# A retention, mixing and gated-MLP kernel: four heads moved to the other half of the partitions, attention's state products in four quarters of the array, and no chunk turned by TensorE

## The chip, the cores and the metric

One core of one Trainium2 chip. The time is device microseconds for one execution of the whole program; lower is better. The kernel before takes 359.83 us (median of three runs, 358.95 to 359.85). The execution that was profiled took 360.07 us, of which 358.3 us lie between its first and its last instruction (the span); the other 1.8 us lie around them. Every time read from the trace counts from the start of the span.

## The reference

Three layers in a row, in float32, for 2 batches of 768 tokens; 8 heads of 64 make 512 features.

```python
def _attn_ref(q, k, v):                      # retention: linear attention with decay
    gamma = 1.0 - 2.0 ** (-5.0 - np.arange(H))
    for t in range(S):
        state = gamma * state + einsum('bhd,bhe->bhde', k[:, :, t], v[:, :, t])
        y[:, :, t] = scale * einsum('bhd,bhde->bhe', q[:, :, t], state)

def _moe_ref(x, w_theta, w_tok_r, w_tok_i, w_ch):
    theta = x @ w_theta
    zr, zi = x * cos(theta), x * sin(theta)
    y = einsum('ts,bsd->btd', w_tok_r, zr) + einsum('ts,bsd->btd', w_tok_i, zi)
    u = x + y
    return u + maximum(u @ w_ch, 0.0)

def _moe2_ref(x, ...):                       # 512 -> 1024, gelu, normed and gated over tokens, -> 512
```

## The kernel before, in words

**Stages.** Retention works on chunks of 128 tokens: 2 batches of 6 chunks, 12 in all. For a chunk, `scores` multiplies keys and queries of each head (contraction over 64 features, so one head uses 64 rows of TensorE's array), `mask` on VectorE copies them out of PSUM, `outer` makes this chunk's k-v product, `grow` (VectorE) and `shrink` (GpSimd) update the state, and `attend` adds up two products: queries with the state so far (only for chunks after the first of a batch: ten of twelve), and masked scores with values. `L682` (VectorE) multiplies the result with the decay `dq` and writes the features `x`. Then `theta` multiplies x with `w_theta`; sine and cosine come from ScalarE. They must be multiplied with x laid out by token, so x is turned: for chunks 0 and 1 (`TURNED`) TensorE transposes it (`turn`, L812); for the other ten, in pairs, VectorE transposes blocks of 32 (`by_token`, L715), one DMA writes them to DRAM (`scr`), and four DMAs bring them back. `mix_main` and `mix_rest` multiply with the token weights; two more stages of matrix products (channels, gated MLP) follow until the end.

**Precision.** The large products run as three fp32r products of high and low parts (`terms3`), so every x, z and weight is split by ScalarE (high part, L349) and VectorE (low part, L355). The small products of retention are plain fp32, and the trace records each of them as two passes: 8 matmuls appear as 16.

**Layout of the heads.** Eight heads are four pairs p; head h (0 or 1) of each pair has its 64 features in partitions 64h to 64h+63, for queries, keys and state alike.

**What sets the order.** `Plan` collects some 1,090 operations; `ORDER`, a list of their numbers, fixes the order in which each engine gets its own. Buffers come from fixed rooms (8 PSUM banks, 36 large SBUF buffers). Where the plan leaves TensorE idle early on, `keep_warm` fills the gap with products of `ident`. SP issues all loads in that order, and at most eight are under way.

Of the kernel before, what the change touches and what calls it, by code (L numbers as in the profile page):

```python
# [19 lines left out]
P = 128  # L20
NCH = S // P
NP = H // 2
# [19 lines left out]
TURNED = (0, 1)  # L42
# [26 lines left out]
class Plan:  # L69
# [171 lines left out]
def retention_spectral_gmlp(  # L241
# [286 lines left out]

    xhl, at = {}, {}
    zhl, z32 = {}, {}  # L530

    def retention(i):
# [12 lines left out]
        for pairs in steps:  # L545
            lo, hi = pairs[0] * P, (pairs[-1] + 1) * P

            def scores(pairs=pairs):
                for p in pairs:
                    for h in range(2):  # L550
                        rows = slice(h * D, (h + 1) * D)
                        cols = slice(p * P, (p + 1) * P)
                        q, k = part_of(qk, 0, p), part_of(qk, 1, p)
                        mm(ap(sc[h])[:, cols], k[rows], q[rows], True, True)
# [46 lines left out]
        if c < NCH - 1:  # L601
            kp = bank()

            def outer(pairs):
                for p in pairs:
                    for h in range(2):
                        rows, cols = slice(h * D, (h + 1) * D), slice(h * D, (h + 1) * D)
                        kk, vv = part_of(kv, 0, p), part_of(kv, 1, p)
                        mm(ap(kp)[rows, p * D : (p + 1) * D], kk[:, cols], vv[:, cols], True, True)
# [33 lines left out]
        xp = bank()  # L643

        def attend(pairs):
            a = ap(at[i])
            if c > 0:
                for p in pairs:
                    cols = slice(p * P, (p + 1) * P)
                    for h in range(2):  # L650
                        rows = slice(h * D, (h + 1) * D)
                        mm(
                            ap(xp)[rows, cols],
                            state[rows, p * D : (p + 1) * D],
                            part_of(qk, 0, p)[rows],
                            p == 0,
                            False,
                        )
# [911 lines left out]
```

## Time and profile before

| | |
|---|---|
| time, median of 3 | 359.83 us |
| the profiled execution | 360.07 us |
| its span | 358.3 us |
| TensorE busy | 353.4 us (99%) |
| VectorE busy | 286.0 us (80%) |
| ScalarE busy | 222.3 us (62%) |
| granted TensorE clock, mean | 1.000 (the 2.4 GHz level) |

Busy time is the union of an engine's instructions; those of TensorE are pipelined, so a pass lasts longer than the distance to the next. For prices the distance from the start of one run of equal passes to the start of the next is used below.

### The profile page before, as it was taken

What the parts mean: (1) busy time and instruction counts of PE and PEld (TensorE: products, weight loads), DVE (VectorE), ACT (ScalarE), POOL (GpSimd) and SP (SyncE); (2) the same over time, 40 slices, a digit from 0 to 9 for tenths busy, and PEclk for the clock granted to TensorE, in tenths of its full rate; (3) what the DMA queues carried; (4) which work ended last, traced back from release to release, by engine and by line L of the source; (5) the groups of instructions that cost most, each with busy time, mean ns of one, the idle gap of its engine ahead of it and who ended that gap; (6) DMA issues with size and microseconds to landing.
All of it is one profiled execution on the core that took longest, in us unless ns stands there. A gap on an engine that the chain in (4) does not pass through costs nothing.

```text
span 358.3 us, 5888 instructions
## 1 busy us (share of the span) xinstructions
PE 353.4 (99%) x2294; PEld 303.0 (85%) x2294; DVE 286.0 (80%) x468; ACT 222.3 (62%) x368; POOL 35.8 (10%) x47
## 2 busy tenths in 40 slices
PE   8999999999999999999999999999999999999996
PEld 8887887778899888889989888888888888999885
DVE  2799997989674786619799986989899794997993
ACT  2768976658561787484768679675698549236300
POOL 1111020000300030013021301000000003100000
PEclk9999999999999999999999999999999999999999
DMA  7999999149609056907559802911000015600344
GB/s 302 411 416 408 368 281 301 20 169 361 218 10 330 16 127 139 292 5 126 107 109 292 143 15 45 307 31 31 0 0 2 1 29 91 105 12 8 80 151 172
DMA packets 18123, 54.04 MB, mean 151 GB/s; under 512 B 2224, under 2 KB 5808, under 8 KB 15664
## 3 DMA queue, kind: packets, MB, share of 16 engines
q1 hardware_dynamic: 13776, 43.92, 34.3%
q0 software_dynamic: 4176, 9.70, 15.4%
q8 instruction: 18, 0.29, 0.3%
q14 instruction: 9, 0.07, 0.1%
q10 hardware_dynamic: 144, 0.05, 0.1%
HBM read 38.19 MB, written 5.77 MB: 123 GB/s over the span
## 4 chain that ended last, share of the span: by engine, by line
PE 89%; DMA 4%; DVE 4%; ACT 1%; issue 1%; DVEq 0%; SPq 0%
PE banks L329 89%; DMA b<-qkv 3%; DMA b<-wts 2%; DVE b L355 1%; DVE b L834 1%; ACT b L788 0%; DVE b L563 0%; DVE b L460 0%; DVE b L777 0%; PE banks L812 0%; ACT b L349 0%; DVE b L715 0%; DVE xa L682 0%; ACT b L795 0%; DVE b L581 0%
## 5 line engine op out<-in xcount | busy, mean ns | idle before, releaser
L329 PE MATMUL banks<-b,b 128*128 128x512 f32 (+2 forms) x1752 | 320.6, 350 | 0.4 <-DVE xa L682 0.4
L329 PEld LDWEIGHTS banks<-b,b 128*128 128x128 f32 (+1 forms) x1752 | 271.8, 183 | 46.8 <-issue 2.1
L349 ACT ACTIVATE b<-b 128x512 fp32r<-128x512 f32 (+1 forms) x95 | 69.8, 756 | 39.2 <-PE banks L329 12.8
L355 DVE TENSOR_TENSOR b<-b,b 128x512 fp32r<-128x512 f32 (+1 forms) x66 | 54.8, 846 | 15.2 <-ACT b L349 10.9
L378 POOL DMA_DIRECT2D b<-b x29 | 25.0, 971 | 186.9 <-ACT b L373 163.6
L436 ACT ACTIVATE b<-b 128x1024 f32<-128x1024 f32 x16 | 18.5, 1153 | 9.8 <-DMA b<-wts 9.8
L373 ACT ACTIVATE b<-b 128x512 fp32r<-128x512 f32 (+1 forms) x29 | 20.8, 736 | 4.1 <-PE banks L329 2.8
L349 ACT ACTIVATE b<-xa 128x512 fp32r<-128x512 f32 (+1 forms) x24 | 16.0, 666 | 10.7 <-PE banks L329 4.8
L563 DVE TENSOR_TENSOR b<-banks,causal 128x512 f32<-128x512 f32 x24 | 15.7, 684 | 5.8 <-PE banks L329 5.7
L329 PE MATMUL banks<-b 64*128 64x128 f32 (+1 forms) x352 | 19.9, 260 | 0.0
L1011 ACT ACTIVATE b<-b 128x512 f32<-128x512 f32 x24 | 14.6, 624 | 8.4 <-DVE b L1001 8.3
L329 PEld LDWEIGHTS banks<-b 64*128 64x128 f32 (+1 forms) x352 | 17.9, 170 | 2.0 <-issue 0.9
L586 ACT ACTIVATE b<-b,dec 128x64 f32<-128x64 f32 x56 | 14.0, 337 | 7.8 <-DMA b<-qkv 7.7
L355 DVE TENSOR_TENSOR b<-xa,b 128x512 fp32r<-128x512 f32 (+1 forms) x24 | 17.5, 729 | 0.2
L630 POOL TENSOR_TENSOR state<-grown,dec 128x256 f32<-128x256 f32 x8 | 6.9, 864 | 107.2 <-DVE grown L627 95.7
L834 DVE TENSOR_TENSOR b<-b,b 128x512 f32<-128x512 f32 x20 | 13.2, 684 | 5.0 <-ACT b L795 3.4
L1172 DVE SCALAR_TENSOR_TENSOR b<-banks,gcol,brow 128x512 f32<-128x512 f32 x12 | 8.9, 746 | 6.3 <-PE banks L329 6.3
L993 ACT ACTIVATE b<-banks 128x512 f32<-128x512 f32 x18 | 10.3, 586 | 4.7 <-PE banks L329 2.5
L1017 DVE SCALAR_TENSOR_TENSOR b<-b,banks 128x512 f32<-128x512 f32 x18 | 12.2, 676 | 1.2 <-ACT b L1011 1.2
L452 ACT ACTIVATE b<-b 128x1024 int32<-128x1024 uint8 x11 | 12.3, 1131 | 1.2 <-DMA b<-wts 1.2
L1001 DVE SCALAR_TENSOR_TENSOR b<-b,banks 128x512 f32<-128x512 f32 x18 | 12.0, 677 | 1.2 <-ACT b L993 1.2
L1102 ACT ACTIVATE b<-b,rstd 128x512 f32<-128x512 f32 x12 | 9.3, 808 | 5.7 <-DVE rstd L1091 5.7
(80 smaller groups left out, 264.1 us busy)
## 6 DMA issues: line engine op xcount, KB each, us to landing
b<-wts SPq DMA_DIRECT2D x16, 1024.0 KB, 6.9
b<-qkv SPq DMA_DIRECT2D x24, 512.0 KB, 9.9
b<-b POOLq DMA_DIRECT2D x21, 256.0 KB, 4.3
b<-b POOLq DMA_DIRECT2D x8, 512.0 KB, 5.5
out<-b SPq DMA_DIRECT2D x11, 256.0 KB, 2.3
scr<-b SPq DMA_DIRECT2D x5, 512.0 KB, 3.4
b<-scr SPq DMA_DIRECT2D x20, 128.0 KB, 6.9
b<-wsg SPq DMA_DIRECT2D x9, 256.0 KB, 6.9
```

The lines of the kernel that those rows point to most:

```text
L329: nc.tensor.matmul(out=o, lhsT=l, rhs=r, start=start, stop=stop, skip_group_check=more)
L349: act(words, lambda: A.activation(out=hi(), in_=src(), func=AF.Copy), prio=prio, r=r, **k)
L355: lambda: E.tensor_tensor(out=lo(), in0=src(), in1=hi().bitcast(F32), op=ALU.subtract),
L373: lambda: A.activation(out=ap(l, F32R), in_=src(), func=AF.Copy, scale=-1.0),
L378: lambda: G.dma_start(out=ap(l, F32R), in_=src(), accum_op=ALU.add),
L436: lambda: A.activation(out=words(1).bitcast(F32), in_=words(1).bitcast(F32), func=AF.Prelu, scale=REBIAS, alpha=SIGN_UP,),
L452: lambda: A.activation(out=words(0), in_=top(), func=AF.Copy, scale=1 / 32, bias=-31 / 64),
L563: V.tensor_tensor(out=ap(at[i])[:, h * 512 + lo : h * 512 + hi].rearrange("p (n t) -> p n t", n=n), in0=ap(sc[h])[:, lo:hi].rearrange("p ( ...
L586: A.activation(out=v, in_=v, func=AF.Copy, scale=dk[:, h : h + 1])
L834: V.tensor_tensor(out=v, in0=x, in1=v, op=ALU.mult)
L1011: lambda: A.activation(out=ap(s), in_=ap(s), func=AF.Tanh, scale=GA * GC),
L1017: lambda: V.scalar_tensor_tensor(out=ap(o), in0=ap(s), scalar=1.0, in1=ap(t), op0=ALU.add, op1=ALU.mult),
```

## The change

Three edits and a new order.

1. Pairs 2 and 3 (the latter four heads) get their queries, keys and state with the two heads swapped between the partition halves: `rows_of` gives half `h ^ (p // 2)`. The host lays the data out so (`feat`, `_decays`).
2. `attend` adds up in two PSUM banks instead of one, one for pairs 0 and 1 and one for pairs 2 and 3, and takes the pairs in the order 0, 2, 1, 3 for the products with the state. Four such products in a row then have the four combinations of input half and output half. The multiplication with `dq` is cut in two, one for each bank.
3. `TURNED` is empty: chunks 0 and 1 are turned by VectorE and DRAM like the rest.

```diff
-TURNED = (0, 1)
+TURNED = ()
...
 ORDER = [
-    48, 50, 49, 118, 63, 62, 105, 106, 119, 52, 51, 0, 55, 53, 56, 54, 168, 120, 58, 272, 67, 121,
...
+    48, 50, 63, 49, 64, 51, 0, 115, 114, 52, 179, 128, 65, 53, 129, 55, 54, 56, 66, 6, 68, 58, 57,
...
+    def rows_of(p, h):
+
+        k = h ^ (p // 2)
+        return slice(k * D, (k + 1) * D)
...
                     for h in range(2):
-                        rows = slice(h * D, (h + 1) * D)
+                        rows = rows_of(p, h)
                         cols = slice(p * P, (p + 1) * P)
                         q, k = part_of(qk, 0, p), part_of(qk, 1, p)
-                        mm(ap(sc[h])[:, cols], k[rows], q[rows], True, True)
+                        mm(ap(sc[h ^ p // 2])[:, cols], k[rows], q[rows], True, True)
...
-        xp = bank()
-
-        def attend(pairs):
+        xp = [bank(), bank()]
+
+        def attend():
             a = ap(at[i])
+
+            def out(p, h):
+                cols = slice(p % 2 * P, (p % 2 + 1) * P)
+                return ap(xp[p // 2])[h * D : (h + 1) * D, cols]
+
             if c > 0:
-                for p in pairs:
-                    cols = slice(p * P, (p + 1) * P)
+                for p in (0, 2, 1, 3):
                     for h in range(2):
-                        rows = slice(h * D, (h + 1) * D)
+                        rows = rows_of(p, h)
                         mm(
-                            ap(xp)[rows, cols],
-                            state[rows, p * D : (p + 1) * D],
-                            part_of(qk, 0, p)[rows],
-                            p == 0,
-                            False,
+                            out(p, h), state[rows, p * D : (p + 1) * D],
+                            part_of(qk, 0, p)[rows], p % 2 == 0, False,
                         )
...
-                        a[:, h * 512 + p * P : h * 512 + (p + 1) * P],
+                        a[:, (h ^ p // 2) * 512 + p * P :][:, 0:P],
...
-        dve(
-            512,
-            lambda: V.tensor_tensor(
-                out=x_chunk(i),
...
+        for e in range(2):
+
+            def fade_q(e=e):
+                V.tensor_tensor(
+                    out=x_chunk(i)[:, 2 * e : 2 * e + 2],
+                    in0=ap(xp[e])[:, 0:256].rearrange("p (n t) -> p n t", n=2),
+                    in1=dq[:, e * 256 : (e + 1) * 256].rearrange("p (n t) -> p n t", n=2),
+                    op=ALU.mult,
+                )
+
+            dve(256, fade_q, ps=True, r=[xp[e], "dq"], w=keys[2 * e : 2 * e + 2], prio=t + 5)
```

The new `ORDER` moves operations on every engine. Two places matter for what follows. First TensorE, the last rows up to its first product with `w_theta`. Before (scores are `128x128` from one buffer; outer `64x64`; products with the state `64x128` with `state`; with values the other `64x128`; turning is L812; theta `128x512`):

```order
L329 MATMUL banks<-b_115 64x64 x8
L329 MATMUL banks<-b_113,state_66 64x128 x8
L329 MATMUL banks<-b_236,b_115 64x128 x8
L329 MATMUL banks<-b_117 64x64 x8
L329 MATMUL banks<-b_107,state_67 64x128 x8
L329 MATMUL banks<-b_175,b_117 64x128 x8
L329 MATMUL banks<-b_146 128x128 x8
L329 MATMUL banks<-b_164 128x128 x8
L329 MATMUL banks<-b_178 128x128 x8
L812 MATMUL banks<-ident,xa_88 128x128 x4
L329 MATMUL banks<-b_328,b_282 128x512 x2
L329 MATMUL banks<-b_341,b_282 128x512
```

With the change, up to the same product:

```order
L330 MATMUL banks<-b_106,state_67 64x128 x8
L330 MATMUL banks<-b_158,b_110 64x128 x8
L330 MATMUL banks<-ident 128x128 x4
L330 MATMUL banks<-b_116 128x128 x8
L330 MATMUL banks<-b_114 64x64 x8
L330 MATMUL banks<-b_129 128x128 x8
L330 MATMUL banks<-b_116,state_66 64x128 x8
L330 MATMUL banks<-b_262,b_114 64x128 x8
L330 MATMUL banks<-b_131 128x128 x8
L330 MATMUL banks<-b_260,b_194 128x512 x2
L330 MATMUL banks<-b_291,b_194 128x512
```

Before, theta begins when seven chunks have scores, four have an outer product and four are attended; with the change, when five have scores, three an outer product and three are attended. Of the fillers `ident` there were 5 matmuls (3 and 2) and there are 12 (3, 3, 2 and 4), the last four of them ahead of the third chunk's scores, which need the load of `b_116`.

Second SP's queue from its start, before:

```order
L517 DMA b_111<-qkv 128x1024
L517 DMA b_113<-qkv 128x1024
L517 DMA b_115<-qkv 128x1024
L517 DMA b_117<-qkv 128x1024
L542 DMA dq<-qdecays 128x512
L425 DMA xb<-wts 128x2048
L517 DMA b_146<-qkv 128x1024
```

These follow four other loads of `qkv`. With the change, from the first load:

```order
L518 DMA b_103<-qkv 128x1024
L518 DMA b_106<-qkv 128x1024
L518 DMA b_108<-qkv 128x1024
L518 DMA b_110<-qkv 128x1024
L548 DMA dq<-qdecays 128x512
L426 DMA xb<-wts 128x2048
L518 DMA b_114<-qkv 128x1024
L518 DMA b_116<-qkv 128x1024
```

`dq` and the first half of `w_theta` (`xb`, 1 MB) go ahead of the third chunk's two loads (`b_114` keys and values, `b_116` queries and keys, 0.5 MB each); before, eight loads of `qkv` went ahead of them.

## Rows read from the trace of the kernel before

**Rows 1.** The page: engines' busy time; DMA share in 40 slices of 9 us.

```profile
PE 353.4 (99%) x2294; PEld 303.0 (85%) x2294; DVE 286.0 (80%) x468; ACT 222.3 (62%) x368; POOL 35.8 (10%) x47
...
DMA  7999999149609056907559802911000015600344
```

**Rows 2.** The page: the chain that ended last, by engine.

```profile
PE 89%; DMA 4%; DVE 4%; ACT 1%; issue 1%; DVEq 0%; SPq 0%
```

**Rows 3.** TensorE's timeline: start, length, operation, passes, [idle before].

```profile
7.07 0.71 PE L329 MATMUL banks<-ident 128*128 128x128 f32 x4
7.71 1.78 PE L329 MATMUL banks<-b 128*64 128x64 f32 x32
...
20.30 2.95 PE L329 MATMUL banks<-b 64*128 64x128 f32 x48
23.18 0.65 PE L812 MATMUL banks<-ident,xa 128*128 128x128 f32 x4
23.59 5.73 PE L329 MATMUL banks<-b,b 128*128 128x512 f32 x24
29.25 1.09 PE L329 MATMUL banks<-b,state 64*64 64x128 f32 x16
30.27 1.09 PE L329 MATMUL banks<-b,b 128*64 128x128 f32 x16
31.20 0.63 PE L329 MATMUL banks<-b 128*64 128x64 f32 x16
31.76 3.02 PE L329 MATMUL banks<-b,b 128*128 128x512 f32 x12
34.71 1.16 PE L329 MATMUL banks<-b 64*128 64x128 f32 x16
35.80 1.09 PE L329 MATMUL banks<-b,state 64*64 64x128 f32 x16
...
61.13 15.49 PE L329 MATMUL banks<-b,b 128*128 128x512 f32 x66 [0.23 <-DVE xa L682]
...
80.92 29.27 PE L329 MATMUL banks<-b,b 128*128 128x512 f32 x167 [0.20 <-DVE xa L682]
```

**Rows 4.** TensorE's groups by shape: the products with the state.

```profile
L329 PE MATMUL banks<-b,state 64*64 64x128 f32 x160 | 10.9, 275 | 0.0
```

**Rows 5.** ScalarE's timeline: the fourth load's values faded; the first weight load's first use.

```profile
8.45 2.02 ACT L586 ACTIVATE b<-b,dec 128x64 f32<-128x64 f32 x8 [5.94 <-DMA b<-qkv]
...
17.88 1.17 ACT L436 ACTIVATE xb<-xb 128x1024 f32<-128x1024 f32 x1 [0.19 <-DMA xb<-wts]
```

**Rows 6.** Busy time by window: PE, PEld, DVE, ACT, POOL, PEclk, DMA share, GB/s.

```profile
30.00:40.00 10.00, 10.00 (x126) 8.41 (x121) 9.81 (x17) 9.50 (x22) 0.99 (x1) 1.00 1.02 410
```

**Rows 7.** VectorE's timeline: steps by size, and the first mixing product's low part.

```profile
7.24 1.29 DVE L563 TENSOR_TENSOR b<-banks,causal 128x512 f32<-128x512 f32 x2 [0.72 <-PE banks L329]
...
18.52 0.41 DVE L627 TENSOR_TENSOR grown<-banks,state 128x256 f32<-128x256 f32 x1
18.85 0.69 DVE L460 TENSOR_SCALAR xb<-xb 128x1024 int32<-128x1024 int32 x1
...
27.07 1.21 DVE L483 SCALAR_TENSOR_TENSOR xa<-xa 128x1024 int32<-128x1024 int32 x1
28.20 1.28 DVE L563 TENSOR_TENSOR b<-banks,causal 128x512 f32<-128x512 f32 x2
29.40 0.70 DVE L715 STREAM_TRANSPOSE b<-xa 128x512 f32<-128x512 f32 x1
30.03 1.18 DVE L355 TENSOR_TENSOR b<-xa,b 128x1024 fp32r<-128x1024 f32 x1
...
51.69 1.21 DVE L355 TENSOR_TENSOR b<-b,b 128x1024 fp32r<-128x1024 f32 x1
```

More of the change, by code (lines that the diff above doesn't have):

```diff
@@ L606, in outer @@
                     for h in range(2):
-                        rows, cols = slice(h * D, (h + 1) * D), slice(h * D, (h + 1) * D)
+                        rows, cols = rows_of(p, h), slice(h * D, (h + 1) * D)
                         kk, vv = part_of(kv, 0, p), part_of(kv, 1, p)
@@ L650, in attend @@
                     for h in range(2):
-                        rows = slice(h * D, (h + 1) * D)
+                        rows = rows_of(p, h)
                         mm(
-                            ap(xp)[rows, cols],
-                            state[rows, p * D : (p + 1) * D],
-                            part_of(qk, 0, p)[rows],
-                            p == 0,
-                            False,
-                        )
-            for p in pairs:
-                cols = slice(p * P, (p + 1) * P)
+                            out(p, h), state[rows, p * D : (p + 1) * D],
+                            part_of(qk, 0, p)[rows], p % 2 == 0, False,
+                        )
@@ L661, in attend @@
+            for p in range(NP):
                 for h in range(2):
-                    rows = slice(h * D, (h + 1) * D)
                     mm(
-                        ap(xp)[rows, cols],
+                        out(p, h),
                         part_of(kv, 1, p)[:, h * D : (h + 1) * D],
-                        a[:, h * 512 + p * P : h * 512 + (p + 1) * P],
+                        a[:, (h ^ p // 2) * 512 + p * P :][:, 0:P],
                         c == 0,
-                        c == 0 or p == NP - 1,
+                        c == 0 or p % 2 == 1,
@@ L669, in attend @@
                     )
-        for pairs in steps:
-            r = [*faded(pairs), (at[i], 0, pairs[0]), (at[i], 1, pairs[0])]
-            if c > 0:
-                r += [*landed(qk), ("state", c % 2)]
-            pe(
-                (0.93 if c == 0 else 1.95) / share, named(attend, pairs),
-                form="attend", r=r, w=[(xp, pairs[0])], prio=t + 3,
-            )
-        keys = [("x", b, c, d) for d in range(NP)]
-        dve(
-            512,
-            lambda: V.tensor_tensor(
-                out=x_chunk(i),
-                in0=ap(xp).rearrange("p (n t) -> p n t", n=NP),
-                in1=dq.rearrange("p (n t) -> p n t", n=NP),
-                op=ALU.mult,
-            ),
-            ps=True,
-            r=[*((xp, x[0]) for x in steps), "dq"],
-            w=keys,
-            prio=t + 5,
-        )
+        r = [*faded(), (at[i], 0, 0), (at[i], 1, 0)]
@@ new lines, in retention @@
+        if c > 0:
+            r += [*landed(qk), ("state", c % 2)]
+        pe(0.93 if c == 0 else 1.52, attend, form="attend", r=r, w=xp, prio=t + 3)
+        keys = [("x", b, c, d) for d in range(NP)]
+        for e in range(2):
[7 more added lines that the diff above has]
+            dve(256, fade_q, ps=True, r=[xp[e], "dq"], w=keys[2 * e : 2 * e + 2], prio=t + 5)
@@ L1498, in _decays @@
     dk = g ** -t[:, None]
-    dk = np.concatenate([dk, rows**P, np.zeros((P, 96 - H - NP))], axis=1)
+    gone = rows**P
+    gone[:, 2:] = np.roll(gone[:, 2:], D, axis=0)
+    dk = np.concatenate([dk, gone, np.zeros((P, 96 - H - NP))], axis=1)
     return dk.astype(np.float32), dq.reshape(P, NP * P).astype(np.float32)
@@ L1518, in feat @@
         a = a.reshape(B, NP, 2, NCH, P, D).transpose(0, 3, 2, 5, 1, 4)
-        return a.reshape(B, NCH, P, 512)
+        a = a.reshape(B, NCH, P, 512).copy()
+        a[..., 256:] = np.roll(a[..., 256:], D, axis=2)
+        return a
     def toks(a):
```

115 rows, old and new, of the table ORDER are left out of this document.

## The prediction

> **What bounds the kernel now.** I read the busy times first, then the chain that ended last, then TensorE's timeline. TensorE is busy 99% of the span, VectorE 80% [rows 1], and 89% of the chain runs through TensorE [rows 2]. The timeline shows the same in detail: runs of passes follow each other without a gap, and in the whole of it there are two idle spells after the start, 0.23 us at 61.13 and 0.20 us at 80.92, both ended by VectorE work on x [rows 3]. So a microsecond taken from TensorE's passes is a microsecond off the end, as long as the others still deliver in time. They are close behind early on: from 30 to 40 us VectorE is busy 9.81 of 10 us, ScalarE 9.50, and the DMA engines are full at 410 GB/s [rows 6]; the DMA share stays at 9 tenths until about 62 us [rows 1]. The early stretch is therefore where the change must be costed with care: TensorE is the bound there, with three near-bounds under it.
>
> **The products with the state.** They are 160 passes, ten runs of 16 [rows 4]. One run takes from 29.25 to 30.27, 1.02 us. What does one pass cost? 48 score passes take 2.88 us (20.30 to 23.18), 16 take 1.09 (34.71 to 35.80), so 32 more take 1.79: 56 ns each. Four passes of the same 128 columns over the whole array, the turn at 23.18, take 0.41, about 100 ns each [rows 3]. So small passes already run two at a time, in steps of 0.11 us; a state run is eight such steps and 0.14 us of coming in and leaving. With four quarters at work it is four steps: 0.58 us, 0.44 saved, 4.4 in ten runs.
>
> Whether four quarters do work at once no row shows. Two rows show the parts: scores use two halves of the rows, each over all columns and into a bank of its own, and the products with values at 30.27 use all rows for two halves of the columns with two different inputs, 16 passes in 0.93 us [rows 3]. The change needs both together. The bounds are 0 and 4.4; I take 4.4, since each part is shown at the full factor of two.
>
> The Trainium skill has a rule that speaks against it: "TensorEngine Tiling (Array Packing)", section Restrictions and Gotchas, says that different row tiles cannot access the same PSUM bank simultaneously. Here heads 0 and 1 of a pair use different rows and write one bank, before and after. By the rule a state run before would go one pass at a time, 16 by 100 ns; the row has 1.02 us for all 16, so the trace does not bear it out for outputs in different partitions. Taken at its word, two banks would allow two at a time and the saving would be 0, as in the first rival below.
>
> **The turn of chunks 0 and 1.** Two runs of 0.41 us leave TensorE [rows 3]: 0.8. In their place VectorE gets four block transposes of 0.63 (29.40 to 30.03) and, for two multiplications of 1024 words (1.13, from 27.07 to 28.20), four of 512 (0.60 each, two from 28.20 to 29.40) [rows 7]: 2.7 us. DMA gets 0.5 MB out and 0.5 MB back, 2.6 us at 410 GB/s [rows 6], in the full stretch.
>
> **The halved multiplication with dq.** 24 steps of 256 words (0.33, from 18.52 to 18.85) for 12 of 512 (0.60) [rows 7]: 0.7 us more of VectorE. In all VectorE gets 3.4 us more; if nothing hid it, the gain would shrink by as much.
>
> **The start.** Here the new order gives some of it back. The third chunk's scores stand behind seven other loads: four of 0.5 MB, `dq`, 1 MB of `w_theta` and `b_114`. ScalarE began on the fourth 0.5 MB load at 8.45 [rows 5]. At 410 GB/s [rows 6] 0.25 MB take 0.64 us, 1 MB 2.56, and two loads of 0.5 MB 2.56: `b_116` lands at 14.2. But before, the 1 MB load, tenth in the queue, was due by the same count at 16.8, and ScalarE waited for it until 17.88 [rows 5]. What held it by 1.1 us no row says; loads landing after 14 us may all have it. So 14.2 to 15.3; I take 15.3, since the nearest load in time was late. TensorE is there first: the work ahead of it ends near 13.9 with the four fillers (two filler matmuls took 0.64 us at 7.07 [rows 3]). From 15.3 come scores 1.09, outer 0.56, scores 1.09, state 0.58, values 0.93 and 0.1, scores 1.09 [rows 3]: theta starts at 20.8, against 23.59 before, 2.8 us earlier.
>
> It starts with less done. Left over, against the kernel before at its own first theta, are: one attend more (0.58 + 0.93 + 0.1 = 1.6), two scores (2.2), one outer product (0.56, from 31.20 to 31.76); less, one turn (0.41) and the seven state runs that the kernel before still had ahead (7 by 0.44 = 3.1). And more changes of form: 24 large passes took 5.66 us (23.59 to 29.25), 12 took 2.95 (31.76 to 34.71), so 12 more take 2.71, and 0.24 is the price of a block [rows 3]; the new order has nine such blocks among small products, the old one six: 0.7. Sum +1.55. With the 2.8 the end comes 1.25 us earlier. Nothing large is lost on the way: 4.4 and 0.8 are won, and some 3 go to fillers and waiting for loads ahead of theta, 0.7 to changes of form.
>
> **What hides VectorE's extra work.** In the new order 65 VectorE instructions end with the low part of the first z, which the first mixing product reads: by the steps above (29 and 4 fast shifts of 0.60, 18 of 0.33, 6 of 0.63, 8 of 1.13) 38.6 us. In the kernel before 64 did, worth 41.7, begun at 7.24 and ended at 52.9 [rows 7], 4.0 us of it waiting. So after, from 7.24: between 45.8 and 49.8. TensorE asks for it at 49.1 (20.8, then 27 us of small products and theta at the same prices, then six passes). The wait is 0 to 0.7 there; behind it in TensorE's queue stand the mixing products of chunks 0 and 1, so all of it would count. The two waits of before, 0.43 together, stand in the order at other places and I count them as gone, with 0.2 for new ones, near the low end because VectorE's early waits were for TensorE, which now delivers sooner. If the 3.4 us had no cover at all, the wait would be 3.4.
>
> **Sum.** 1.25 + 0.43 - 0.2 = 1.5 us off. The profiled execution of 360.07 becomes 358.6; that execution lies 0.24 over the median of 359.83, so **358.3** for a median.
>
> **Rivals.**
> *The quarters take turns.* Only two passes run at a time, as now. Then a state run keeps 1.02 us and the second bank and the switching buy nothing: 4.4 are missing, 362.7, slower. For it: no row has four at once. Against it: both halves of the mechanism run at full factor in the rows. It decides against the change from the point where a run saves less than 0.3 us of its 0.44. A weaker form, in which a quarter's second pass holds up the next pair and three steps in eight are saved less than fully (0.29 a run), gives 359.8: no change.
> *The second bank is not free.* Each chunk under way holds five of eight banks, before four. If the third state product waits for VectorE to empty a bank, TensorE stands for up to a step of 0.33 to 0.60 [rows 7] in each of ten chunks, 3 to 6 us at the very most; more likely in two to four chunks that run among the mixing products with their four banks: 1 to 2 us, 359.3 to 360.3.
> *The round trip through DRAM is late.* Chunk 0's blocks stand eighteenth in SP's new queue, and five loads of 0.5 MB stand between them and the way back. If they come after VectorE wants them, the first z slips; what lies past 2 us goes onto TensorE's path. Same time range as above. For it the full DMA engines [rows 6], against it that 65 VectorE instructions lie before.
> *The loads come on time.* `b_116` at 14.2, no new waits: 1.1 to 1.3 us better, 357.1.
>
> **How the numbers follow.** Differences under 0.3% (1.1 us) can hardly be told from none. Chances: the forecast 0.45, reaching from 357.8 to 359.0 (0.33 faster, 0.12 same); loads on time 0.17, faster; the weak form of the quarters, a bank or DRAM wait of 1 to 3 us 0.26 (0.05 faster, 0.16 same, 0.05 slower); quarters in turns 0.10, slower, with 0.02 for several waits at once (slower). That is 0.55 faster, 0.28 same, 0.17 slower. The range must leave out no more than 2 in 10: from 356.6, a little under the on-time case, to 360.9, which leaves out the turns and the worst waits. The likeliest case alone: 357.6 to 359.2.
>
> **What would show it.** Right: runs of 16 state passes with about 0.58 us to the next run, no L812, a first theta near 20.8 us, with an idle spell or fillers ahead of the third scores, TensorE without gaps from then on, and VectorE near 289 us busy. Wrong: state runs of 1.0 us (quarters in turns), or 0.73 (the weak form); idle of 0.3 us or more inside state runs (banks); TensorE waiting near 49 us for the multiplication with the turned x (DRAM).

## The result: slower by 0.7%

The changed kernel takes **361.4 us** (median of five, 361.3 to 362.3); the kernel before, run beside it on the same chip, 359.56 (358.67 to 359.85). The ratio is 1.0066, with a 95% interval of 1.0053 to 1.008. The forecast was 358.3, range 356.6 to 360.9, "faster" at 0.55: outside the range and on the wrong side. The profiled execution took 361.61 us, its span is 359.9.

The page of the changed kernel: busy times, DMA share by slice, and the chain that ended last by engine (answers to [rows 1, 2]).

```profile
PE 352.0 (98%) x2300; PEld 298.6 (83%) x2300; DVE 288.9 (80%) x484; ACT 222.2 (62%) x368; POOL 36.3 (10%) x47
...
DMA  7999995934449409937348616701000014703054
...
PE 85%; DMA 10%; DVE 3%; issue 1%; ACT 0%; SPq 0%; DVEq 0%; ACTq 0%
```

The group of all products with the state, by shape (answers to [rows 4]):

```profile
L330 PE MATMUL banks<-b,state 64*64 64x128 f32 x160 | 6.7, 282 | 0.0
```

TensorE's timeline of the changed kernel (start, length, operation, passes, idle before; answers to [rows 3]):

```profile
15.42 2.87 PE L330 MATMUL banks<-b 64*128 64x128 f32 x48 [1.61 <-DMA b<-qkv]
...
20.93 3.01 PE L330 MATMUL banks<-b,b 128*128 128x512 f32 x12
...
27.20 0.67 PE L330 MATMUL banks<-b,state 64*64 64x128 f32 x16
27.80 1.09 PE L330 MATMUL banks<-b,b 128*64 128x128 f32 x16
...
42.59 4.37 PE L330 MATMUL banks<-b,b 128*128 128x512 f32 x18
48.23 1.16 PE L330 MATMUL banks<-b 64*128 64x128 f32 x16 [1.26 <-DMA b<-qkv]
49.32 3.03 PE L330 MATMUL banks<-b,b 128*128 128x512 f32 x12
...
66.90 1.16 PE L330 MATMUL banks<-b 64*128 64x128 f32 x16
...
90.15 5.06 PE L330 MATMUL banks<-b,b 128*128 128x256 f32 x40
```

What the reader is to see: the sought saving is there. The 160 passes with the state take 6.7 us where they took 10.9 [rows 4], and a run goes on to the next after 0.60 us (27.20 to 27.80). The first theta starts at 20.93, forecast 20.8. But TensorE's share of the chain fell from 89% to 85% and DMA's rose from 4% to 10% (4 of the 10 are the loads ahead of 15.42): at 48.23 TensorE had stood 1.26 us for a load of queries and keys (chunk 7's). Next, VectorE's timeline between 71 and 79 us, and the chain at 78 and at 145 us (start, length, what):

```profile
71.74 0.70 DVE L461 TENSOR_SCALAR b<-b 128x1024 int32<-128x1024 int32 x1 [1.27 <-DMA b<-wts]
73.00 1.23 DVE L484 SCALAR_TENSOR_TENSOR b<-b 128x1024 int32<-128x1024 int32 x1 [0.56 <-ACT b L437]
...
78.01 0.42 DVE L684 TENSOR_TENSOR xa<-banks,dq 128x256 f32<-128x256 f32 x1
```

```profile
78.09 0.34 DVE xa L684
...
78.48 1.11 PE banks L330 x17
...
144.83 6.49 DMA b<-scr
...
153.95 1.24 DVE b L356
...
155.23 201.15 PE banks L330 x1031
```

Two more places where a transfer leads: VectorE stands 1.27 us for 1 MB of weights and 0.56 us for ScalarE's work on them, so the multiplication with `dq` (L684) frees a bank late, and TensorE's outer product waits until 78.48; at 144.8 a block read back from DRAM holds the last z. Three stretches of busy time, with clock, DMA share and GB/s (answers to [rows 6]; the last lies within the first):

```profile
30.00:40.00 10.00, 10.00 (x85) 8.11 (x85) 9.95 (x16) 9.21 (x24) 0.98 (x1) 1.00 1.05 356
40.00:50.00 10.00, 8.74 (x85) 7.19 (x84) 10.00 (x16) 8.45 (x15) 0.00 (x0) 1.00 0.94 308
...
36.00:38.00 2.00, 2.00 (x19) 1.42 (x21) 2.00 (x3) 2.00 (x7) 0.00 (x0) 1.00 1.11 233
```

From 30 to 40 the DMA engines are as full as before (1.05 against 1.02) but move 356 GB/s instead of 410 [rows 6]; the lowest of it is the 233 from 36 to 38, while the blocks of chunks 0 and 1 are read back (from 36 to 39 us 476 of 548 packets are under 2 KB).

### The profile page after: what moved, and what is told of

Read it like the earlier page. It is cut to its first block, busy times and chain, and to the rows that moved or that the text cites. A ratio compares the mean times of both kernels' runs of the same rounds, so it can differ in the third digit from the quotient of the medians.

```text
span 359.9 us, 5923 instructions
## 1 busy us (share of the span) xinstructions
PE 352.0 (98%) x2300; PEld 298.6 (83%) x2300; DVE 288.9 (80%) x484; ACT 222.2 (62%) x368; POOL 36.3 (10%) x47
## 4 chain that ended last, share of the span: by engine, by line
PE 85%; DMA 10%; DVE 3%; issue 1%; ACT 0%; SPq 0%; DVEq 0%; ACTq 0%
PE banks L330 85%; DMA b<-qkv 6%; DMA b<-scr 2%; DMA b<-wts 1%; DVE b L356 1%; DMA dec<-decays 1%; DVE b L833 1%; DVE xa L684 0%; ACT b L350 0%; DVE b L776 0%; DVE b L587 0%; DVE b L569 0%; DVE b L1372 0%; SPq L426 0%; DVEq L833 0%
## 5 line engine op out<-in xcount | busy, mean ns | idle before, releaser
L833 DVE TENSOR_TENSOR b<-b,b 128x512 f32<-128x512 f32 x24 | 16.0, 683 | 7.6 <-DMA b<-scr 7.0
L1010 ACT ACTIVATE b<-b 128x512 f32<-128x512 f32 x24 | 14.8, 627 | 10.0 <-DVE b L1000 10.0
L636 POOL TENSOR_TENSOR state<-grown,dec 128x256 f32<-128x256 f32 x8 | 7.9, 984 | 95.4 <-DVE grown L633 95.4
L473 DVE SCALAR_TENSOR_TENSOR b<-b 128x1024 int32<-128x1024 int32 x8 | 9.7, 1213 | 6.9 <-ACT b L437 6.9
L767 ACT ACTIVATE b<-banks 128x512 int32<-128x512 f32 x12 | 6.9, 586 | 13.0 <-PE banks L330 13.0
L787 ACT ACTIVATE b<-b 128x512 f32<-128x512 f32 x12 | 7.4, 623 | 11.4 <-DVE b L776 11.4
```

The source lines that it names most:

```text
L833: V.tensor_tensor(out=v, in0=x, in1=v, op=ALU.mult)
L1010: lambda: A.activation(out=ap(s), in_=ap(s), func=AF.Tanh, scale=GA * GC),
```

## The experiments

**Theory T:** the state products save what was forecast, and the waits for transfers around the added round trip of chunks 0 and 1 take it back. **Rivals:** the four quarters are worth nothing at the end; VectorE's extra steps or the second bank cost the time; or DMA time is simply short, so that whatever stands last is waited for. "Ratio" is against the kernel before, run on the same chip in the same session; its medians in those four sessions were 359.12, 359.36, 359.45 and 359.04, and 359.56 beside the changed kernel. Microseconds of different sessions are therefore uncertain by up to 0.5, and where it matters the difference by the ratios stands beside them.

### Order of the pairs (e1_two_quarters)

```diff
-                for p in (0, 2, 1, 3):
+                for p in (0, 1, 2, 3):
```

> The changed kernel with the passes with the state in the order of pairs 0, 1, 2, 3 instead of 0, 2, 1, 3, so that neighbouring passes use two quarters of the array and not four. Nothing else differs. Theory T (the quarters save what was forecast, and the gain is lost to loads that come later): a state run goes from 0.60 back to about 1.0 us, 0.42 more in each of ten runs, 4.2 in all; the one ahead of the wait at 15.4 and up to 1.4 us of the four ahead of the wait at 46.6 disappear in those waits, so 362.9 to 363.9. Rival (the four quarters give nothing to the end, whatever the rows say): 361.4, no change.

Measured: 361.3 us, ratio 1.0055 (1.0038 to 1.0073), as the changed kernel. This looks like the rival, but the edit did not do what it was made for. TensorE's timeline of this run:

```profile
27.11 0.68 PE L330 MATMUL banks<-b,state 64*64 64x128 f32 x16
27.72 1.09 PE L330 MATMUL banks<-b,b 128*64 128x128 f32 x16
```

A state run still takes 0.61 us. The passes of this run start at 0, 6, 26, 33 and 161 ns (in the changed kernel at 0, 7, 14, 20 and 161): whichever of the two orders the passes are written in, four are under way at once. So the order of the pairs in the change is worth 0.01 us a run, and the experiment tells nothing between the theories. What makes the four quarters is the layout (further down).

### Without the round trip of chunks 0 and 1 (e2_no_round_trip_01)

```diff
-            512, lambda: nc.sync.dma_start(out=scr, in_=ap(tt)), r=[(tt, 0), (tt, 1)],
+            512, lambda: i >= 2 and nc.sync.dma_start(out=scr, in_=ap(tt)), r=[(tt, 0), (tt, 1)],
...
             def move(c=c):
+                if i < 2:
+                    return
...
+                if i < 2:
+                    x = x_chunk(i).rearrange("p d (a k) -> p d a k", a=4)
```

> The changed kernel without the write to DRAM and the four reads back for chunks 0 and 1; their multiplications read the chunk unturned, so this leaves out the turning of chunks 0 and 1. All of VectorE's steps, the order, the banks and every other transfer are kept. Theory T (the extra round trip takes DMA time in the full stretch and makes chunk 7's queries and keys late): that load lands about 2.5 us earlier, the wait of 1.4 us at 46.6 is gone, and part of the 0.6 around 77 to 87 with it: 359.4 to 360.0. Rival (VectorE's extra steps or the second bank are what costs): the waits stay, 361.4.

Measured: 359.49 us, ratio 1.0002 (0.9987 to 1.0018): 1.9 less than the changed kernel (2.3 by the ratios; 1.8 less than the run above, in the same session), as T expected. This kernel leaves out the turning of chunks 0 and 1. The DMA issue of chunk 7's queries and keys in this run (count, size, us to landing), and the windows:

```profile
b<-qkv SPq DMA_DIRECT2D x1, 512.0 KB, 10.7
```

```profile
30.00:40.00 10.00, 10.00 (x84) 8.13 (x82) 9.98 (x16) 9.17 (x24) 0.99 (x1) 1.00 1.02 411
40.00:50.00 10.00, 10.00 (x95) 8.21 (x92) 10.00 (x16) 8.71 (x16) 0.00 (x0) 1.00 0.82 221
```

Issued at 32.68, it lands at 43.4; in the changed kernel it was issued at 38.67 and landed 9.42 us later, at 48.1. So the round trip of 0.5 MB each way holds that load up by 4.7 us, not by the 2.6 that bytes at 410 GB/s give; the stretch moves 411 GB/s again. The changed kernel's trace shows two things behind the price, which were not separated: the low 233 GB/s while the blocks are read back, and the issuing. SP issues in order, and before the four reads it stood for the write to land (waits of SP from 0 to 40 us: total, times, longest), so that nothing was issued until 32.49:

```profile
SPq L731 <- DMA scr<-b: 6.5, 1, 6.5
```

VectorE is as busy as ever (9.98 and 10.00 of 10 us) and TensorE does not wait in the stretch, which speaks against VectorE's extra steps and the bank. A part is lost again later, here in the slowest of the ten executions (360.23), which is the one that was traced. TensorE's and VectorE's timelines:

```profile
154.01 6.18 PE L330 MATMUL banks<-b,b 128*128 128x512 f32 x25 [0.76 <-DVE b L356]
```

```profile
150.23 1.29 DVE L837 TENSOR_TENSOR b<-b,b 128x512 f32<-128x512 f32 x2 [7.80 <-DMA b<-scr]
```

That is the place near 155 where the changed kernel loses time too. It shows without the round trip of chunks 0 and 1 as well, so that round trip alone does not explain it.

### One load sooner (e3_load7_sooner)

```diff
+def sooner(k, ahead_of):
+    ORDER.remove(k)
+    ORDER.insert(ORDER.index(ahead_of), k)
+
+sooner(298, 151)
```

> The changed kernel with one load moved: the queries and keys of chunk 7 are issued ahead of the write to DRAM for chunks 2 and 3 and of the 1 MB of weights behind it, no longer behind both. Theory T: it lands near 42 instead of 48.1, the wait of 1.4 us at 46.6 is gone, the other transfers of the stretch land up to 1.3 us later, and if nobody waits for those the time is 360.0. Rival (the DMA engines are simply full, so that whoever is put last is waited for): another wait of about the same size takes its place, 361.0 to 361.6.

Measured: 360.77 us, ratio 1.0041 (1.0019 to 1.0063), single executions from 359.7 to 362.5. In between: the wait ahead of chunk 7's scores is gone, and two others came. TensorE's timeline in the traced execution, the slowest of the ten (362.46, 1.7 over the median):

```profile
66.37 1.16 PE L337 MATMUL banks<-b 64*128 64x128 f32 x16 [0.82 <-DMA b<-qkv]
...
79.31 0.69 PE L337 MATMUL banks<-b 128*64 128x64 f32 x16 [0.98 <-DVE xa L691]
```

Moving one load is not enough; this run alone leaves T and "DMA time is short" both standing.

### The quarters in the old order (b1_old_order_quarters)

```diff
-TURNED = ()
+TURNED = (0, 1)
 ORDER = [
...
-                keep_warm(idle[0], int((gap - (0.1 if done < 9.0 else 0.5)) / 0.24))
+                idle and keep_warm(idle[0], int((gap - (0.1 if done < 9.0 else 0.5)) / 0.24))
```

The list `ORDER` is too long to show; it is that of the kernel before, with the second half of each multiplication with `dq` behind the first and the places put back that the expectation tells of. The last line leaves a filler out where no bank is free for it.

> The kernel before with the four quarters alone: the latter heads in the other half, two output banks, halved multiplications with dq, but chunks 0 and 1 still turned by TensorE, and the old order of work (each second half of a multiplication right behind its first; 34 places put back by one to six until a bank is free, TensorE's own order unchanged). Were the second bank free of cost: 359.6 less 4.2 is 355.4. If the bank is waited for by one step of VectorE (0.33 to 0.60) in each of twelve chunks: 4 to 7 us come back, 359.4 to 362.6. Theory T names the DMA as what eats the gain of the changed kernel and says nothing against 355.4 here; the bank rival expects 359.4 or more.

Measured: 366.68 us, ratio 1.0194 (1.0151 to 1.0238). The bank rival holds here, and by more than its own range. TensorE's timeline, and a window with the granted clock (the figure before the last two):

```profile
32.03 0.69 PE L330 MATMUL banks<-b 128*64 128x64 f32 x16 [0.98 <-DVE xb L684]
...
53.92 1.12 PE L330 MATMUL banks<-b,state 64*64 64x128 f32 x12 [1.30 <-DVE b L569]
...
61.30 5.03 PE L330 MATMUL banks<-b,b 128*128 128x512 f32 x15 [2.56 <-DVE xa L684]
```

```profile
60.00:64.00 4.00, 2.70 (x7) 2.16 (x8) 3.16 (x7) 0.00 (x0) 0.00 (x0) 0.59 0.52 147
```

A chunk under way holds five of eight banks here, in an order made for four: TensorE waits for VectorE's `dq` step (L684), and around the longest wait the granted clock is 0.59 of full speed, a mixture of its two levels (1.2 and 2.4 GHz); in the two stretches of 4 us before it was 0.74 and 0.83. The longest wait has a second cause: VectorE had stood 1.55 us for weights ahead of that step. It did so in the kernel before too (1.57 us), where TensorE lost only 0.23 at that place [rows 3]. So the quarters do not pay in the old order. What in the new order pays for the second bank, the earlier theta or the small products under way, was not taken apart.

### Four transfers moved (e4_four_loads_moved)

```diff
+sooner(298, 151)
+sooner(428, 321)
+sooner(899, 265)
+sooner(452, 520)
```

In this order: chunk 7's queries and keys ahead of a write to DRAM; 0.5 MB that is wanted late, back; the biases, back; the last of four reads ahead of 1 MB of weights.

> The changed kernel with four transfers moved in SP's queue and nothing else: chunk 7's queries and keys ahead of the write to DRAM for chunks 2 and 3 (as in the run before with that alone); the 0.5 MB that is wanted only at 112 us (issued at 60 ahead of another that is wanted at 64) back to about 90; the row of biases, 384 KB wanted at about 100, behind two loads of weights; and the last of the four reads of chunks 10 and 11 ahead of 1 MB of weights. Theory T (the loss is loads that stand in a bad order around the extra round trips): the waits at 46.6 (1.4 us), 77 to 87 (0.8) and 154.8 (0.5) go, 361.4 less 2.7 is 358.7. Rival (the DMA time itself is short, so the last in the queue is always waited for): new waits of the same size, 360.8 to 361.4.

Measured: 360.72 us, ratio 1.0041 (1.0026 to 1.0056): just under the rival's range, and 2.0 over T's 358.7. The waits that it aimed at are gone from TensorE's timeline; TensorE is 2.1 us earlier than in the changed kernel at its first passes of 256 columns. But a new one stands behind. VectorE's and TensorE's timelines:

```profile
94.58 1.23 DVE L366 TENSOR_TENSOR b<-b,b 128x1024 fp32r<-128x1024 f32 x1 [2.44 <-DMA scr<-b]
...
95.86 1.34 PE L340 MATMUL banks<-b,b 128*128 128x256 f32 x9 [1.52 <-DVE b L366]
```

VectorE wanted to write into the buffer that was still being written to DRAM: the 0.5 MB had been put ahead of that write. A round trip is also a buffer that comes free late.

### The moves refined (e7_moves_refined)

```diff
 sooner(298, 151)
-sooner(428, 321)
-sooner(899, 265)
+sooner(363, 428)
+sooner(428, 259)
+sooner(899, 321)
 sooner(452, 520)
```

Transfer 363 is the 0.5 MB that is wanted sooner; it takes the place of 428.

> The changed kernel with the moves of the run with four transfers moved, set so that nothing stands ahead of the write to DRAM for chunks 6 and 7 and the last 1 MB of weights: the 0.5 MB wanted at 112 goes behind the next 1 MB of weights (issue near 75), the biases behind the weights issued near 83. In the run with four transfers that write landed at 94.5, VectorE stood 2.4 us for its buffer and TensorE 1.7 us at 94. Theory T (the order of the transfers around the extra round trips): that wait goes, the others stay gone, 360.7 less 1.7 is 359.0, and the wait at 15.4 is the only one left over 0.3 us. Rival (DMA time itself is short): another wait of over 1 us appears, 360.3 or more.

Measured: 359.39 us, ratio 0.9998 (0.9982 to 1.0015): 2.0 less than the changed kernel (2.4 by the ratios), near T's 359.0. TensorE has no new wait of 1 us in place of the one at 94. What is left starts in VectorE's timeline, again in the slowest execution (360.24, 0.85 over the median):

```profile
53.75 0.70 DVE L472 TENSOR_SCALAR b<-b 128x1024 int32<-128x1024 int32 x1 [2.48 <-DMA b<-wts]
```

### A fifth move (e10_fifth_move)

```diff
+sooner(42, 154)
```

It puts those weights ahead of the reads that wait for a write.

> The kernel of the refined moves with one transfer more moved: the 1 MB of weights that was issued at 46.0, behind the wait for the write to DRAM of chunks 2 and 3 and three of its four reads, is issued ahead of that wait. In the refined run it landed at 53.7, VectorE stood 2.5 us for it at 51, and TensorE lost 0.8 us around 66 and 0.6 at 55 and 85 behind VectorE. Theory T: it lands near 50, those waits go, 359.4 less 0.9 is 358.5, as without the round trip of chunks 0 and 1. Rival (DMA time itself): the reads or the next loads are late instead, 359.2 or more.

Measured: 358.92 us, ratio 0.9997 (0.9985 to 1.0009) against 359.04 there. By the ratios (0.9997, and 0.9998 for the refined moves) it is level with the run before it: in time the fifth move brings nothing that can be told, and 358.92 lies between T's 358.5 and the rival's 359.2. In the trace it is the changed kernel without waits: behind the load at 15.93 TensorE's timeline has no idle spell, and from there on the chain is TensorE's alone but for VectorE's last step.

```profile
PE 95%; DMA 4%; DVE 0%; issue 0%
```

```profile
21.44 3.02 PE L342 MATMUL banks<-b,b 128*128 128x512 f32 x12
...
43.11 4.37 PE L342 MATMUL banks<-b,b 128*128 128x512 f32 x18
47.41 1.16 PE L342 MATMUL banks<-b 64*128 64x128 f32 x16
48.51 3.70 PE L342 MATMUL banks<-b,b 128*128 128x512 f32 x15
...
66.08 1.16 PE L342 MATMUL banks<-b 64*128 64x128 f32 x16
...
88.39 6.86 PE L342 MATMUL banks<-b,b 128*128 128x256 f32 x55
```

This run is the ruler for the waits. Its span is 357.6 us, so from its first theta to the end it needs 336.2; the changed kernel needs 359.9 - 20.93 = 339.0. **The waits of the changed kernel are 2.8 us** (2.5 by the ratios of the medians). From 42.59 to 49.32 it spends 1.3 more than the ruler from 43.11 to 48.51; from 66.90 to 90.15, 0.9 more than from 66.08 to 88.39; the rest, some 0.5, lies near 155, at the place that shows without the round trip of chunks 0 and 1 as well.

### The moves without the round trip (e9_refined_no_round_trip_01)

The edit is that of the run without the round trip, made on the refined moves.

> The kernel of the refined moves without the write to DRAM and the four reads for chunks 0 and 1 (their multiplications read the chunk unturned, so this leaves out the turning of chunks 0 and 1). Theory T: with the transfers in this order the extra round trip is hidden, and leaving it out changes the time by less than 0.3 us. Rival (DMA time itself): 1 us or more faster.

Measured: 358.5 us, ratio 0.997 (0.9961 to 0.9979), 0.9 less than the refined moves. T's "under 0.3" is wrong, and the rival's "1 us or more" is nearly met: the refined moves had not yet hidden the round trip. The fifth move took away the last waits in the trace without leaving anything out. From first theta to end this run needs 356.4 - 20.46 = 335.9 us, the fifth move 336.2, so in the traces the two differ by their start (a load landed earlier in this one, first theta at 20.46 against 21.44). The earlier start does not come with leaving the round trip out: the first run without it began theta at 21.18. Where the 0.9 us of the medians lies was not settled.

### Two quarters by the layout (e6_two_quarters_layout, e5_moved_two_quarters, e8_refined_two_quarters)

The same edit on the changed kernel, on the four moves, and on the refined moves:

```diff
-        k = h ^ (p // 2)
-        return slice(k * D, (k + 1) * D)
+        return slice(h * D, (h + 1) * D)
...
-                        mm(ap(sc[h ^ p // 2])[:, cols], k[rows], q[rows], True, True)
+                        mm(ap(sc[h])[:, cols], k[rows], q[rows], True, True)
...
-        a[..., 256:] = np.roll(a[..., 256:], D, axis=2)
...
```

> The changed kernel with only the layout put back: two quarters of the array for the products with the state, the banks, the order and the loads as in the changed kernel. Theory T: a state run takes 1.02 us, 0.42 more; of the ten, the one ahead of 15.4 and 1.4 us of the four ahead of the wait at 46.6 hide in those waits, and 0.8 us of the two around 68 to 77 may hide in the waits of 77 to 87: 362.9 to 363.8. Rival: 361.4, no change.

> The same four moves, with the heads in the old layout: the first head of each pair in the first half of the rows and the second in the second half, for all eight, so that the products with the state use two quarters of the array whatever their order; both output banks, the order and VectorE's steps are kept. Theory T: state runs take 1.02 us again, 0.42 more in each of ten runs; the one ahead of 15.4 hides in the wait for a load, so 3.8 us over the run with the moves alone. Rival (what a state run saves is given back by VectorE and the loads that are due sooner): less than 1.5 us over it.

> The kernel of the refined moves with the heads in the old layout, so that the products with the state use two quarters: state runs of 1.02 us. Theory T: 0.42 in nine of the ten runs (the one ahead of 15.4 hides in the wait there), 3.8 us over the refined moves. If the later arrival of TensorE also covers waits that are left, less: down to 3.3. Rival (the quarters' saving is given back): under 1.5.

Measured: on the changed kernel 363.22 us (ratio 1.011, 1.009 to 1.013), 1.8 more (1.6 by the ratios); on the refined moves 362.71 (1.0093, 1.0075 to 1.011), 3.3 more; on the four moves 366.16 (1.0184, 1.0161 to 1.0207), 5.4 more. TensorE's timeline of the first:

```profile
28.11 1.09 PE L330 MATMUL banks<-b,state 64*64 64x128 f32 x16
29.14 1.09 PE L330 MATMUL banks<-b,b 128*64 128x128 f32 x16
```

State runs take 1.03 us again, and their passes start two at a time (at 0, 6, 161 and 166 ns). The first two times are within what T expected and far from "no change": the four quarters are worth 3.3 us where little else waits, and in the changed kernel only 1.8 of it, since the waits swallow the rest (its wait ahead of chunk 7's scores is gone from this trace). The third is off T's 3.8. There TensorE's wait near 97 grew to 2.21 us, and behind it the clock fell:

```profile
99.36 21.19 PE L340 MATMUL banks<-b,b 128*128 128x256 f32 x118 [2.21 <-DVE b L366]
```

```profile
100.00:104.00 4.00, 4.00 (x15) 3.42 (x15) 1.98 (x3) 0.00 (x0) 1.29 (x2) 0.57 0.75 214
```

None of the kernels that compute the whole beats the kernel before beyond its interval; the fifth move equals it.

## Why the prediction was wrong, point by point

**The state products: right.** 0.58 us a run was forecast, 0.60 measured, 4.2 us in ten runs. "The quarters take turns" and its weak form fall: the first four passes of a run start within 20 ns, the next at 161. The Trainium skill, "TensorEngine Tiling (Array Packing)", section Restrictions and Gotchas, says that different row tiles cannot access one PSUM bank at the same time. The trace does not agree for outputs in different partitions: heads 0 and 1 of a pair use different rows and one bank, and the run of 16 passes takes 0.60 us, four at a time.

**The start: right.** The third chunk's queries landed at 15.37 (forecast 15.3), the first theta began at 20.93 (20.8). To hit it that closely is partly luck: the 1.1 us by which loads are late was taken over without a cause, and with the same queue up to there theta began between 20.46 and 21.44 in the traces of the new order with four quarters.

**What is left at the first theta: a little small.** Before, 358.3 - 23.59 = 334.7 us followed, 0.43 of it the two waits: 334.3 of work. The ruler has 336.2 without waits: 1.9 more, where 1.55 was forecast. The 0.35 between them was not taken apart.

**VectorE: right.** 288.9 us busy (289 forecast), and no wait for z at 49; the first mixing product began six passes after 49.32.

**The step that failed** is the last line of the working: "the two waits of before, 0.43 together ... I count them as gone, with 0.2 for new ones". In place of 0.2 stand 2.8 us, 1.3 of them ahead of chunk 7's scores, 0.9 around 78 to 87 and 0.5 near 155. The round trip was costed at 2.6 us of DMA time "in the full stretch" and then left out of the sum, as if a full queue could take it for nothing. It took 4.7, and it was not the turned blocks that came late, which the DRAM rival looked at, but the loads queued behind them: chunk 7's queries and keys, then weights. The 0.5 near 155 are the reads of a later pair, which come late in the run without that round trip too. The DRAM rival named the right transfer and the wrong victim, and so a price of 1 to 2 us. Moving these transfers takes all these waits out of the trace with the round trip kept, and brings 2.4 us by the ratios already in the refined moves. So the order of the queue was the cause of most of them rather than the sum of bytes. The rival that DMA time is simply short does not explain these waits, but it is not dead: in the refined order leaving the round trip out is still worth 0.9 us, and e3 and e4 show that moving one or four can merely move the wait.

**The second bank: right for the new order.** Its only trace in the changed kernel is the late outer product at 78.48, which follows from the late weights. In the old order the rival is real: the waits on VectorE's steps and the lower clock cost more than the quarters bring.

**The base.** The forecast took the profiled execution of before as 0.24 us over its median. The five medians on record since, on different chips, lie between 359.04 and 359.56; against these it was 0.5 to 1.0 over, and even without its waits the changed order could be no more than level with before or a little under it: 358.9 against 359.0 is what the fifth move shows.

**The sum made good.** 358.6 for a profiled execution, plus 2.6 of waits, 0.3 of work and 0.1 of start, is 361.6; 361.61 was measured. The terms are differences of the same spans, so the sum has to close; it shows where the miss lies and is no further evidence.

## What to carry to other kernels

When DMA engines are full, cost an added transfer by the next loads in the same queue: ask for each when it is wanted, and add the transfer's whole time to its landing: the time as measured, with the wait of a read for its write, and not bytes over the peak rate (here 4.7 us against 2.6). Then look for what can be put behind it; here the moved transfers took every new wait out of the trace. And test an edit's mechanism in the trace before reading its time: the order of the pairs changed neither the runs' length nor the time, while the layout changed both.

## What the runs showed of the hardware

Passes into different quarters need not be neighbours in program order to run at once: 0.61 us for a state run with pairs 0, 1, 2, 3, 0.60 with 0, 2, 1, 3, in both with four starts within 33 ns. A round trip of 0.5 MB through DRAM, written in one transfer and read in four of 128 KB, held up a load behind it by 4.7 us, and the full engines moved 356 GB/s from 30 to 40 us instead of 411, 233 from 36 to 38. Around TensorE's waits of 2.56 us (old order) and 2.21 us (four moves, two quarters) the granted clock was 0.59 and 0.57 over 4 us; with the four moves alone, where the wait was 1.52 us, the trace shows 1.00 over the 4 us behind it. In the old order the clock was at 0.74 already from 52 to 56 us, where TensorE waited 0.31 and 1.30 us.
